# Values of ten column blocks in seven products of quarters, in the second and third batch of a routed attention followed by a gated feed-forward layer

## The chip, the cores and the metric

The kernel runs on one core of a Trainium2 chip. The metric is the device time of one execution in microseconds, the median of three runs. The engines are PE (matmul; PEld is its weight load), DVE (vector), ACT (scalar), POOL (GpSimd) and SP, which here only issues DMAs. PE, DVE and ACT reach the matmul accumulators (PSUM, eight banks); POOL works on SBUF alone.

## The reference

Four batches of eight heads with 768 tokens of 64 numbers. Each query and key goes to the nearest of 16 centroids of its head, and a query attends only to keys of its own cluster. The result, 3072 tokens of 512 numbers, goes through a feed-forward layer of 1536 columns with a sigmoid gate.

```python
q_assign = np.argmax(np.einsum('bhsd,hcd->bhsc', q_n, c_n), axis=-1)
k_assign = np.argmax(np.einsum('bhsd,hcd->bhsc', k_n, c_n), axis=-1)
mask = q_assign[:, :, :, None] == k_assign[:, :, None, :]
scores = np.where(mask, scale * np.matmul(q, k.transpose(0, 1, 3, 2)), -1e9)
attn = softmax(scores)
x = (attn @ v).transpose(0, 2, 1, 3).reshape(B * S, H * D)
gate = 1.0 / (1.0 + np.exp(-(x @ w_gate)))
out = (gate * (x @ w_val)) @ w_out
```

## The kernel before

The program writes out the order of the work by hand. It walks through 384 attention steps, 96 a batch, 24 for each pair of heads and 12 for each head. A step is one score matmul of a key chunk against half the queries (128x384, L1066), one exponential on ACT (L1071), and three small matmuls with the values (av, 128x65, L1089) for the step two places back. `at(step, f)` puts other work at a step: loads of k, q and v (`load`), their splits into a high and a low half-precision part (`sp`, L1631 on DVE, L1632 on POOL), the turn of the split tile by DMA (`turn`), the logits, the pick of the cluster and the hops of the one-hot rows (`pair_prep`). These run some 40 to 80 steps ahead of the head's use.

The feed-forward layer of a batch runs beside the attention of the next. Its pieces ("atoms") stand in a queue, each with a nominal cost in ns; `ffn_run` lets a step take atoms for `ns` (a number for each quarter of a batch in the table `SCHED`). In the first three batches `ffn_atoms` makes them: for each half of the tokens (`blk`, 384 tokens) and each of twelve column blocks `fc` of 128, a gate (four matmuls of 128x384 over the four parts of the 512, then tanh on ACT into `th`) and a value (four matmuls, then one DVE operation (th + 1) * v into `hT`, L553). Sigmoid comes as half of tanh of the half plus a half; the factors sit in the weights' scale. From the second batch on the out product is done for pairs of token chunks in seven products of quarters in place of eight (`product_out`, L994, with sums of `hT` made by `Sums.make` on DVE). The first pair m0 is put `aside` when the first half's values are done, and its atoms alternate with the second half's gates and values; the pairs (3, 2) and (4, 5) follow.

The last batch has no attention behind it. `closing` computes gates and values of ten column blocks in seven products of quarters (columns in pairs, tokens in halves, the 512 in halves): `fin_weights` makes four differences of weight quarters on DVE, `fin_tokens` four sums of token quarters, a `Unit` does the seven products of a pair of column blocks; partial sums are copied from PSUM by ACT, added by DVE, and multiplied with the gate by POOL (L708).

PSUM: a `ring` of four banks (scores, gates, values, logits), two av banks, and two `op` banks, which `out_bank` hands out in turn. `product_out` takes both and chooses by `taken["last"]` which of them its first product writes:

```python
slot = taken["op"] % 2
u = [out_bank() for _ in range(2)]
x = 0 if slot != taken["last"] else 1
taken["last"] = (slot + x) % 2
for z, t in (("x", u[x]), ("y", u[1 - x])): ...
```

SBUF: load tiles `kraw`, `qraw`, `vraw` three each, split tiles `hl` four, turned tiles `T` eight, `th` three.

Of the kernel before, what the change touches and what calls it, by code (L numbers as in the profile page):

```python
# [8 lines left out]
FP = mybir.dt.float32  # L9
# [86 lines left out]
    "fwv": [354, 356, 357, 359, 364, 366, 370, 371], "b3p2pk1": -28.5, "END": 0,  # L96
# [4 lines left out]
def kernel(  # L101
# [42 lines left out]
    hlp = pool("hl", 4)  # L144
    hl2p = pool("hl2", 2)
    tp = pool("T", 8)
# [38 lines left out]
    ident = const.tile([128, 128], FP, name="ident")  # L185
# [12 lines left out]

    def raw(side, b, p):
# [15 lines left out]
    cen = const.tile([128, D], FP, name="cen")  # L215
# [64 lines left out]
    c2 = const.tile([128, 2, D], FP, name="c2")  # L280
    sq = const.tile([128, D], FP, name="sq")
# [114 lines left out]
    T = {}  # L396

    def split(n, parts, lo_eng):

        hl = hlp.tile([128, n, 128], HP, tag="hl", name="hl")  # L400
        for o, r in parts:
            DVE.tensor_copy(hl[:, o : o + r.shape[1], 0:64], r)
        for o, r in parts:
            m = r.shape[1]
            lo_eng.tensor_tensor(
                hl[:, o : o + m, 64:128], r, hl[:, o : o + m, 0:64], ALU.subtract
            )
        return hl

    def turn(key, hl, pl):  # L410
        T[key] = pl.tile([128, hl.shape[1], 128], HP, tag="T", name="T")
        SP.dma_start_transpose(out=T[key], in_=hl.rearrange("p c x -> p (c x)"))
# [19 lines left out]
    def logits1(groups, copy=None):  # L432
# [10 lines left out]
        lo = smp.tile([128, 12, NCL], FP, name="lglo")  # L443
# [134 lines left out]
    def fin_room():  # L578
        if not fin:
            for x in "kq":  # L580
                for n in range(3):
                    r = rawp.tile([128, 2, NCH, 64], FP, tag=f"{x}raw", name=f"{x}raw", bufs=3)
                    fin[x, n] = r.rearrange("p a c d -> p (a c d)").bitcast(HP).rearrange(
                        "p (h x) -> p h x", h=2
                    )

    def fin_weights(w, i, t):

        fin_room()
        if w == 1 and ("h", 0) not in fin:  # L590
            for n in range(4):
                fin["h", n] = hlp.tile([128, 12, 128], HP, tag="hl", name="hl").rearrange(
                    "p c x -> p (c x)"
                ).rearrange("p (h x) -> p h x", h=2)
        a = FC0 // 2 if i == 0 else 0
        q = lambda k, j: (wg, wv)[w][i][:, 2 * k : 2 * k + 2].rearrange(
            "p d (q j) f -> p d q j f", j=2
        )[:, :, a:, j]
        tw = lambda t: (fin["h", 2 * i + (t - 1) // 2] if w else fin["kq"[i], (t - 1) // 2])[
            :, (t - 1) % 2  # L600
        ].rearrange("p (d q f) -> p d q f", d=2, q=3)
        fin["T", w, i, t] = tw(t)
        z, x, y = {
            1: (tw(1), q(0, 1), q(0, 0)), 2: (tw(2), q(1, 1), tw(1)),
            3: (tw(3), q(1, 1), q(0, 1)), 4: (tw(4), q(1, 0), tw(2)),
        }[t]
        cut = lambda v: v if v.shape[2] == 3 - a else v[:, :, a:]
        DVE.tensor_tensor(cut(z), cut(x), cut(y), ALU.subtract)

    def fin_tokens(xT, t):  # L610

        fin_room()
        s = lambda t: fin["kq"[(t - 1) // 2], 2][:, (t - 1) % 2].rearrange("p (d x) -> p d x", d=2)
# [3 lines left out]
        need(*(("x", B - 1, p, c) for p in ps for c in cs))  # L617
# [4 lines left out]
        DVE.tensor_tensor(z, x, y, o)  # L622

# [27 lines left out]
    def closing(xT):  # L651
# [9 lines left out]
        slot = []  # L661
        for _ in range(8):
            t = tp.tile([128, 12, 128], HP, tag="T", name="T")
            v = t.rearrange("p c x -> p (c x)").bitcast(FP)
            slot += [v[:, 0:384], v[:, 384:768]]
# [12 lines left out]
        class Unit:  # L678
            def __init__(u, w, n, f):
                u.w, u.f, u.i, u.q = w, f, f // WQ, f % WQ // 2  # L680
                if w:
                    u.c1, u.c12, u.c22 = slot[3 * (n % 2) : 3 * (n % 2) + 3]
                else:
                    u.c22, u.c21 = slot[6 + 2 * (n % 2) : 8 + 2 * (n % 2)]
                    u.c1, u.c12 = slot[10 + 2 * (n % 3) : 12 + 2 * (n % 3)]

            def mm(u, o, k, start, stop):
                T_ = lambda t, d: fin["T", u.w, u.i, t][:, d, u.q, :]
                W_ = lambda k_, j, d: (wg, wv)[u.w][u.i][:, 2 * k_ + d, (u.f + j) % WQ, :]
                A_ = lambda i, k_, d: xT[:, 2 * k_ + d, 384 * (1 - i) : 384 * (2 - i)]  # L690
                S_ = lambda t, d: fin["S", t][:, d]
                for d in range(2):
                    l, r = {
# [317 lines left out]

    def ffn_block(*a):
        queue.extend(ffn_atoms(*a))

    credit = [0.0]
    turn_ = [0]

# [753 lines left out]
```

## Time and profile before

| | us |
|---|---|
| median of three runs | 319.07 |
| lowest and highest | 319.00, 319.25 |
| the profiled execution | 319.12 |
| its span in the trace | 317.3 |
| PE, DVE, ACT, POOL busy | 310.0, 238.6, 244.9, 120.9 |

A group's row reads: line, engine, operation, output <- inputs, shapes, count | busy us, mean ns of one | idle time of the engine before them and what ended it. Busy time is a union: operations of one engine overlap a little, so the next one costs less than a lone one lasts. The first batch's feed-forward runs from about 39 to 128 us, the second's gates and values from 128.6 to 185.2, its out products to 200.2; the third's from 200.2 to 257.7 and 271.7; then comes the closing.

### The profile page before, as it was taken

The page shows a single profiled execution, that of the slowest core. Times are in us where ns is not written, and L with a number is a line of the kernel's source. Part 1 is how long each engine was busy: PE and PEld are TensorE (multiplying, and loading weights), DVE is VectorE, ACT ScalarE, POOL GpSimd, SP SyncE. Part 2 cuts the span into 40 slices and gives each one's busy share as a digit, 9 for nine tenths or more (in the row PEclk, how much of TensorE's full clock was granted, in tenths as well). Part 3 has the DMA queues.
Part 4 walks back from the last instruction along what each step waited for, and adds up shares of the span by engine and source line. Part 5 has one row for each costly group of instructions (what it writes and reads, how often), then busy time and mean ns, then how long its engine had stood idle before and what let it go on. Part 6 is the DMA issues. An engine that isn't in the chain of part 4 may idle for free.

```text
span 317.3 us, 9228 instructions
## 1 busy us (share of the span) xinstructions
PE 310.0 (98%) x3492; PEld 218.8 (69%) x3492; DVE 238.6 (75%) x623; ACT 244.9 (77%) x555; POOL 120.9 (38%) x157
## 2 busy tenths in 40 slices
PE   7899999999999999999999999999999999999995
PEld 4688766766666666666777678766677678656685
DVE  5899756778688777686788688776888776678983
ACT  6688998797899887877776876777877887588621
POOL 5888454244434275423234333424212111026600
PEclk9999999999999999999999999999999999999999
DMA  7999998639848988976676455882506130300014
GB/s 196 379 259 169 271 164 143 176 83 264 242 100 163 204 221 136 199 217 161 106 193 153 151 118 134 248 153 53 112 2 76 55 27 14 145 1 3 0 35 165
DMA packets 77996, 45.16 MB, mean 142 GB/s; under 512 B 56896, under 2 KB 75520, under 8 KB 77952
## 3 DMA queue, kind: packets, MB, share of 16 engines
q1 hardware_dynamic: 73840, 39.66, 51.3%
q0 software_dynamic: 3680, 4.72, 9.1%
q8 instruction: 27, 0.44, 0.6%
q10 hardware_dynamic: 432, 0.20, 0.2%
q14 instruction: 17, 0.14, 0.1%
HBM read 28.34 MB, written 6.29 MB: 109 GB/s over the span
## 4 chain that ended last, share of the span: by engine, by line
PE 93%; DMA 2%; DVE 1%; POOL 1%; SPq 1%; issue 0%; ACT 0%; DVEq 0%
PE sc L1066 19%; PE g L532 15%; PE v L548 15%; PE av L1089 11%; PE o L994 9%; PE o L865 5%; PE lg L436 2%; PE o L699 2%; PE o_end L802 2%; PE av L699 2%; DMA kraw<-in_k_dram 2%; PE v L628 2%; PE y L699 2%; PE o L802 1%; PE av L802 1%; PE z L699 1%
## 5 line engine op out<-in xcount | busy, mean ns | idle before, releaser
L1071 ACT ACTIVATE es<-sc 128x384 f16<-128x384 f32 x384 | 174.1, 492 | 38.5 <-PE sc L1066 29.8
L1066 PE MATMUL sc<-T 128*128 128x384 f16 x384 | 117.3, 325 | 0.7 <-DVE T L1396 0.4
L1089 PEld LDWEIGHTS <-es 128*128 128x128 f16 x1152 | 81.3, 98 | 35.1 <-ACT es L1071 0.2
L1089 PE MATMUL av<-va,es 128*128 128x65 f16 x1152 | 97.6, 194 | 0.0
L553 DVE SCALAR_TENSOR_TENSOR hT<-th,v 128x384 f16<-128x384 f32 x72 | 39.8, 553 | 33.8 <-PE av L1089 29.6
L377 POOL TENSOR_TENSOR xp<-t,rec 128x384 f16<-128x384 f32 (+1 forms) x30 | 21.8, 726 | 97.3 <-DVE rec L374 49.2
L548 PE MATMUL v<-xTb,wv 128*128 128x384 f16 x288 | 58.5, 326 | 0.1
L532 PE MATMUL g<-xTb,wg 128*128 128x384 f16 x288 | 58.5, 326 | 0.0
L538 ACT ACTIVATE th<-g 128x384 f32<-128x384 f32 x72 | 35.4, 492 | 8.3 <-PE g L532 6.3
L1066 PEld LDWEIGHTS <-T 128*128 128x128 f16 x384 | 37.0, 96 | 1.2 <-DVE T L1396 0.7
L548 PEld LDWEIGHTS <-wv 128*128 128x128 f16 x288 | 28.0, 97 | 13.9 <-issue 0.3
L532 PEld LDWEIGHTS <-wg 128*128 128x128 f16 x288 | 27.9, 97 | 13.9
L1632 POOL TENSOR_TENSOR hl<-kraw,hl 128x384 f16<-128x384 f32 x22 | 20.2, 920 | 40.6 <-DVE hl L1631 25.9
L1632 POOL TENSOR_TENSOR hl<-qraw,hl 128x384 f16<-128x384 f32 x22 | 21.1, 961 | 11.1 <-DVE hl L1631 11.1
L865 PE MATMUL o<-wo,hT 128*128 128x512 f16 x72 | 19.9, 379 | 0.0
L372 DVE TENSOR_TENSOR t<-av,sv 128x390 f32<-128x390 f32 (+1 forms) x30 | 14.4, 480 | 7.1 <-PE av L1089 5.3
L941 DVE TENSOR_TENSOR ob<-o,ob 128x256 f32<-128x256 f32 (+1 forms) x28 | 15.0, 549 | 4.7 <-PE o L994 3.2
L708 POOL TENSOR_TENSOR hT<-T 128x384 f16<-128x384 f32 x12 | 11.8, 1001 | 16.2 <-DVE T L657 15.6
L994 PE MATMUL o<-wo,hT 128*128 128x256 f16 x108 | 16.8, 272 | 0.0
L994 PEld LDWEIGHTS <-sum 128*128 128x128 f16 x144 | 14.0, 97 | 3.3
L451 DVE TENSOR_REDUCE lgs<-lg 128x192 f32<-128x384 f32 x23 | 12.7, 551 | 3.0 <-PE lg L436 2.9
L324 POOL CAST va<-vraw 128x768 f16<-128x768 f32 x15 | 13.1, 873 | 2.4 <-DMA vraw<-in_v_dram 2.4
(225 smaller groups left out, 470.2 us busy)
## 6 DMA issues: line engine op xcount, KB each, us to landing
vraw<-in_v_dram SPq DMA_DIRECT2D x15, 384.0 KB, 4.9
kraw<-in_k_dram SPq DMA_DIRECT2D x14, 384.0 KB, 4.2
qraw<-in_q_dram SPq DMA_DIRECT2D x12, 384.0 KB, 4.1
out_dram<-ob SPq DMA_DIRECT2D x17, 256.0 KB, 2.2
wg<-in_moe_w_gate_dram POOLq DMA_DIRECT2D x2, 768.0 KB, 9.2
wv<-in_moe_w_val_dram POOLq DMA_DIRECT2D x2, 768.0 KB, 10.4
wo<-in_moe_w_out_dram POOLq DMA_DIRECT2D x2, 768.0 KB, 9.3
T<-ohT SPq DMA_DIRECT2D x44, 24.0 KB, 1.9
```

Of the source, the lines that this page charges most:

```text
L377: (eng or POOL).tensor_tensor(x, t[:, 0:nq, 0:64], bcast(rec[:, 0:nq], 64), ALU.mult)
L532: PE.matmul(out=g[:, 0:n], lhsT=wg[fc // WQ][:, dc, fc % WQ, :], rhs=xT[:, dc, t0 : t0 + n], start=(dc == 0), stop=(dc == NDC - 1),)
L538: ACT.activation(th[:, 0:n], g[:, 0:n], AF.Tanh)
L548: PE.matmul(out=w[:, 0:n], lhsT=wv[fc // WQ][:, dc, fc % WQ, :], rhs=xT[:, dc, t0 : t0 + n], start=(dc == 0), stop=(dc == NDC - 1),)
L553: DVE.scalar_tensor_tensor(HB[b, blk][:, fc, 0:n], st[0][:, 0:n], 1.0, w[:, 0:n], ALU.add, ALU.mult)
L699: PE.matmul(out=o, lhsT=l, rhs=r, start=start and d == 0, stop=stop and d == 1, skip_group_check=True,)
L865: PE.matmul(out=o, lhsT=HB[b, blk][:, fc, bass.ts(t, 128)], rhs=wo[fc // WON][:, fc % WON, :], start=(fc == 0), stop=(fc == NFC - 1),)
L994: PE.matmul(out=st[z][:, e], lhsT=a[:, c, :], rhs=rhs[:, c, :], start=start and c + e == 0, stop=c == HF - 1, skip_group_check=True,)
L1066: PE.matmul(out=sc.rearrange("p (c t) -> p c t", t=128), lhsT=s["k"], rhs=s["q"], start=True, stop=True,)
L1071: ACT.activation(es, sc, AF.Exp, scale=SCALE)
L1089: PE.matmul(out=av[:, a0 + s["c0"] + i, :], lhsT=s["es"][:, bass.ts(i, 128)], rhs=VA[b, p][:, e, s["j"], :], start=(first and i == 0 and a ...
L1632: POOL.tensor_tensor(hl[:, :, 64:128], r, hl[:, :, 0:64], ALU.subtract)
```

## The change

The second and third batch (b = 1 and 2) get their feed-forward atoms from a new function `middle`. Gates stay whole. Values of the column blocks 0 and 1 stay whole. The other ten are done in five units of two columns as seven products of quarters, with `quarter`, which is `Unit.mm` taken out of the closing. V(f, k) is product k of the unit that begins at column f; x and y are its two `op` banks, z a ring bank. `early` is queued where the first half's atoms were, `late` where the second half's were; m0's out product is no longer put aside but follows the last value.

```diff
+    def middle(xT, b):
+        gcost, pcost = NDC * 384 / 2.4 + 3, 2 * 163.0
+        c12, c22, c1 = home("c")
+        ths = {}
+        def gate(fc, blk):
+            def f():
...
+                g = fin_group(xT, 0, fc, blk)
+                th = ths[fc, blk] = thp.tile([128, 384], FP, name="th")
+                ACT.activation(th, g, AF.Tanh)
+                if fc >= FC0 and (fc % 2, blk) != (0, 0):
+                    POOL.tensor_scalar(th, th, 1.0, None, ALU.add)
+            return (gcost, f)
+        def from_bank(fc, blk, v):
+            DVE.scalar_tensor_tensor(HB[b, blk][:, fc], ths[fc, blk], 1.0, v, ALU.add, ALU.mult)
...
+        def value(f, k):
+            st = units.setdefault(f, {})
+            def out(c, z, j, blk):
+                DVE.tensor_tensor(c, z, c, ALU.add)
+                POOL.tensor_tensor(HB[b, blk][:, f + j], c, ths[f + j, blk], ALU.mult)
+            def g():
+                if k == 1:
+                    taken["pair"] = True
+                    st["x"] = out_bank()[:, 0:384]
+                if k == 5:
+                    st["y"] = out_bank()[:, 0:384]
+                o = bank(512, name="z")[:, 0:384] if k == 2 else st["y" if k in (5, 3) else "x"]
+                quarter(xT, 1, f, o, k, k in (1, 2, 5), True)
+                if k in (1, 6, 7):
+                    ACT.activation({1: c1, 6: c12, 7: c22}[k], o, AF.Copy)
+                if k == 2:
+                    out(c1, o, 0, 1)
+                if k == 7:
+                    out(c22, st["y"], 1, 0)
+                if k == 3:
+                    out(c12, o, 1, 1)
+                if k == 4:
+                    from_bank(f, 0, o)
+            return (pcost, g)
...
+        G, V = (lambda f, j, i: gate(f + j, 1 - i)), value
+        early = [
+            gate(0, 0), val(0, 0), gate(1, 0), val(1, 0), G(6, 1, 1), V(6, 1), G(6, 0, 1), V(6, 5),
+            V(6, 6), V(6, 7),
+        ]
+        late = [(0.0, lambda: fin_tokens(xT, 4, b)), G(6, 0, 0), V(6, 2), V(6, 4), G(6, 1, 0), V(6, 3)]
+        late += [gate(0, 1), val(0, 1), gate(1, 1), val(1, 1)]
+        for f in (2, 8, 4, 10):
+            late += [
+                V(f, 1), G(f, 0, 0), V(f, 5), V(f, 6), V(f, 2), G(f, 1, 1), V(f, 7), G(f, 0, 1),
+                V(f, 4), G(f, 1, 0), V(f, 3),
+            ]
+            if f == 8:
+                late += [part(m, i, 0, 4) for m in (m0, ma) for i in (1, 2, 3)]
+        late += [part(m, i, 4) for m in (m0, ma) for i in (1, 2, 3)]
+        outs = product_out(b, [m0])
+        n = 6 * HF // SCHED.get("og", 3)
+        late += outs[:n] + [part(mb, i) for i in (1, 2, 3)] + outs[n:] + product_out(b, [ma, mb])
+        return early, late
```

To hold the value differences from the second batch on, tiles are given up: load tiles of k and q become two and one (`x`, for the third pair), split tiles two (`hl`) and two (`hx`, first two batches), turned tiles seven and one (`Tx`), and small constants share one tile `misc`, which later serves as the buffer c1. The weight differences are made in halves, and the values' at steps 150 to 178 in place of 354 to 371. The budgets of the steps are lowered.

```diff
-    -1, "b1lv1": 0.5, "b1lv2": 0.5, "b1lv3": 1.5, "ns02": 490, "ns03": 490, "ns20": 500,
-    "ns21": 491, "ns22": 481, "ns23": 410, "ns30": 443, "ns31": 443, "ns32": 443, "ns33": 423,
+    -1, "b1lv1": 0.5, "b1lv2": 0.5, "b1lv3": 1.5, "ns02": 490, "ns03": 490, "ns20": 484,
+    "ns21": 475, "ns22": 466, "ns23": 400, "ns30": 420, "ns31": 420, "ns32": 420, "ns33": 400,
...
-    "fwv": [354, 356, 357, 359, 364, 366, 370, 371], "b3p2pk1": -28.5, "END": 0,
+    "fwv": [150, 154, 158, 162, 166, 170, 174, 178], "b3p2pk1": -28.5, "fs3": 30, "END": 0,
+    for k, s_ in enumerate(SCHED["fwv"]):
...
-    hlp = pool("hl", 4)
+    hlp = pool("hl", 2)
+    hxp = pool("hx", 2)
     hl2p = pool("hl2", 2)
-    tp = pool("T", 8)
+    lop = pool("lo", 2)
+    tp = pool("T", 7)
+    txp = pool("Tx", 1)
...
+        if side != "v":
+            x = b < 2 and p == 2
+            return rawp.tile(
+                [128, 2, NCH, 64], FP, tag=f"{side}raw" + "x" * x, name=f"{side}raw", bufs=2 - x
+            )
...
+    def home(x):
+        if x not in homes:
+            if x in ("k", "q"):
...
+            elif x in ("kx", "qx"):
...
+            elif x == "v":
+                homes[x] = [flat(p.tile([128, 12, 128], HP, tag=p.name, name="wvs"), 3) for p in (txp, hxp, hxp)]
+                homes[x] += [flat(lop.tile([128, 12, NCL], FP, name="lglo"), 3).bitcast(HP) for _ in range(2)]
+            else:
+                homes[x] = [
+                    hl2p.tile([128, 2, 3, 128], HP, tag="hl2", name="hl2").rearrange(
+                        "p a c x -> p (a c x)"
+                    ).bitcast(FP) for _ in range(2)
+                ] + [misc]
+        return homes[x]
...
-        DVE.tensor_tensor(cut(z), cut(x), cut(y), ALU.subtract)
+        for d in range(2):
+            DVE.tensor_tensor(z[d], x[d], y[d], ALU.subtract)
...
+    def quarter(xT, w, f, o, k, start, stop):
+        i, qn = f // WQ, f % WQ // 2 - (FC0 // 2 if f < WQ else 0)
...
+        for d in range(2):
+            l, r = {
+                1: lambda: (W_(0, 0, d), A_(0, 0, d)), 2: lambda: (W_(1, 0, d), A_(0, 1, d)),
+                3: lambda: (W_(1, 1, d), S_(4, d)), 4: lambda: (T_(4, d), A_(1, 1, d)),
+                5: lambda: (T_(1, d), S_(1, d)), 6: lambda: (T_(2, d), S_(2, d)),
+                7: lambda: (T_(3, d), S_(3, d)),
+            }[k]()
+            PE.matmul(
+                out=o, lhsT=l, rhs=r, start=start and d == 0, stop=stop and d == 1,
+                skip_group_check=True,
+            )
...
+                if b in MID:
+                    at(u + lag, lambda xT=xT, b=b, i=i: middle_block(xT, b, i))
+                    if i == 0:
+                        at(u + SCHED.get(f"ms{b}", 9), lambda xT=xT, b=b: [fin_tokens(xT, t, b) for t in (1, 2, 3)])
+                    continue
```

More of the change, by code (lines that the diff above doesn't have):

```diff
@@ L396, with turn @@
     T = {}
[L398 to L411, printed above, removed]
+    def turn(key, hl):
+        T[key] = new_T(*key)
         SP.dma_start_transpose(out=T[key], in_=hl.rearrange("p c x -> p (c x)"))
@@ L576 @@
     fin = {}
[L578 to L585, printed above, removed]
-    def fin_weights(w, i, t):
[L589 to L594, printed above, removed]
-        a = FC0 // 2 if i == 0 else 0
[L596 to L602, printed above, removed]
+    flat = lambda t, n: t.rearrange("p a c d -> p (a c d)" if n == 4 else "p c x -> p (c x)")
@@ L616, in fin_tokens @@
         ps, cs = {1: ((2, 3), (0, 1, 2)), 2: ((), ()), 3: ((0, 1), range(6)), 4: ((2, 3), range(3, 6))}[t]
-        need(*(("x", B - 1, p, c) for p in ps for c in cs))
+        need(*(("x", b, p, c) for p in ps for c in cs))
         z, x, y, o = {
@@ L660, in closing @@
         seq = [*first, lambda: fin_tokens(xT, 4)]
[L661 to L665, printed above, removed]
+        slot = {}
+        room = list(home("c"))
+        for _ in range(7):
+            v = tp.tile([128, 12, 128], HP, tag=tp.name, name="T")
+            v = v.rearrange("p c x -> p (c x)").bitcast(FP)
+            room += [v[:, 0:384], v[:, 384:768]]
+        for n, t in zip((10, 11, 6, 7, 0, 1, 2, 8, 9, 12, 13, 3, 4, 5, 14, 15), room):
+            slot[n] = t
         sums = {x: Sums(b, *x) for x in ((0, 1), (3, 2), (4, 5))}
```

121 lines of the change are left out of this document (80 added, 41 removed).

## The prediction

> **What bounds the kernel now.** I read the page's busy times and slices first, then the chain of waits, then the busy times of five stretches.
>
> ```profile
> PE 310.0 (98%) x3492; PEld 218.8 (69%) x3492; DVE 238.6 (75%) x623; ACT 244.9 (77%) x555; POOL 120.9 (38%) x157
> ...
> PE   7899999999999999999999999999999999999995
> ...
> PE 93%; DMA 2%; DVE 1%; POOL 1%; SPq 1%; issue 0%; ACT 0%; DVEq 0%
> ```
> ```profile
> 128.60:185.20 56.60, 56.53 (x603) 38.70 (x602) 41.80 (x110) 43.43 (x100) 18.11 (x21) 1.00 0.72 170
> 185.20:200.20 15.00, 15.00 (x197) 12.66 (x195) 12.46 (x31) 11.13 (x23) 6.32 (x8) 1.00 0.53 134
> 200.20:257.70 57.50, 57.50 (x608) 39.42 (x606) 43.76 (x110) 46.24 (x105) 14.22 (x18) 1.00 0.44 86
> 257.70:271.70 14.00, 14.00 (x167) 11.84 (x164) 10.76 (x24) 10.49 (x22) 1.56 (x3) 1.00 0.31 56
> 271.70:300.00 28.30, 28.30 (x179) 17.24 (x177) 22.44 (x47) 21.28 (x48) 11.97 (x13) 1.00 0.07 25
> ```
>
> The columns of the second view are the stretch, its length, then PE, PEld, DVE, ACT and POOL with their instruction counts, the granted clock, and DMA. The first and third stretch hold the gates and values of the second and third batch beside the attention of the batch behind them; the second and fourth mainly their out products; the fifth the closing, which already runs the last batch's gates and values as seven products. PE is busy in all of them at clock 1.00, and the chain is PE for 93% of the span. So a matmul taken out is worth its issue time, if the others keep up. In the first stretch DVE has 26% free, ACT 23%, POOL 68%: this is what the change spends.
>
> **Prices.** From the timeline and the chain:
>
> ```profile
> 200.46 0.65 PE g L532 x4
> ```
> ```profile
> 207.64 0.81 PE L548 MATMUL v<-xTb,wv 128*128 128x384 f16 x4
> ...
> 208.56 0.55 DVE L553 SCALAR_TENSOR_TENSOR hT<-th,v 128x384 f16<-128x384 f32 x1 [0.81 <-PE v L548]
> ...
> 210.49 0.32 PE L1066 MATMUL sc<-T 128*128 128x384 f16 x1
> ...
> 210.74 0.32 PE L1066 MATMUL sc<-T 128*128 128x384 f16 x1
> ```
> ```profile
> 152.65 0.87 ACT L1071 ACTIVATE es<-sc 128x384 f16<-128x384 f32 x2 [0.29 <-PE sc L1066]
> ```
>
> Four 128x384 matmuls take 0.65 us of the chain: 0.163 each. An attention step without a product (one score, three av) takes 210.74 - 210.49 = 0.25 us. DVE starts 208.56 - 208.45 = 0.11 us behind the last matmul that it reads. Two ACT operations end 0.87 us after the first began and one lasts 0.49, so the next one costs 0.38.
>
> **What the change removes.** Per batch ten of the twelve value blocks, in five units of two. A unit had 2 blocks x 2 token halves x 4 matmuls = 16 of 128x384 and now has 7 products x 2 = 14. Ten units lose 20 matmuls: 20 x 0.163 = **-3.26 us** of PE. Nothing else on PE changes in number.
>
> **What it adds on ACT.** Three copies a unit, 30 in all:
>
> ```profile
> L1071 ACT ACTIVATE es<-sc 128x384 f16<-128x384 f32 x74 | 34.2, 491 | 9.4 <-PE sc L1066 8.2 <-PE av L1089 1.0
> L538 ACT ACTIVATE th<-g 128x384 f32<-128x384 f32 x24 | 11.8, 493 | 3.7 <-PE g L532 3.0 <-DVE t L372 0.2 <-DVE hl L1631 0.2
> ```
>
> A unit takes 30 matmuls (14 product, 16 gate) x 0.163 = 4.9 us, plus, at the planner's 0.42 to 0.48 us of products a step, some 11 steps x 0.25 = 2.8: 7.7 us. ACT has 11 exponentials + 4 tanh + 3 copies = 18 x 0.38 = 6.8 us of that, 89%. It hides, but a late copy now holds the exponentials queued behind it, and the av matmuls wait for those.
>
> **What it adds on POOL.** Three products a unit, like the closing's, and three additions of 1.0 to a gate, which the trace doesn't show:
>
> ```profile
> L708 POOL TENSOR_TENSOR hT<-T 128x384 f16<-128x384 f32 x12 | 11.8, 1001 | 16.2 <-DVE T L657 15.6 <-ACT T L758 0.6
> ...
> L1287 POOL CAST hl<-kraw 128x384 f16<-128x384 f32 x2 | 1.0, 499 | 0.0
> ```
>
> An addition costs between the one-input cast, 0.50 us, and the two-input product, 1.00; I take 0.50, since it reads one tensor. A unit then costs POOL 3 x 1.0 + 3 x 0.5 = 4.5 us, and the work already there 18.11/56.60 x 7.7 = 2.5: 7.0 of 7.7 us in the second batch (91%), 14.22/57.50 x 7.7 + 4.5 = 6.4 in the third (83%). What is late when POOL is late: the buffers c1, c12, c22 have one copy each. ACT's copy after product 6 overwrites c12, which POOL must have multiplied since the last unit's product 3. In the changed order V1, G, V5, V6 stand between them: 14 matmuls and about 3 steps, some 3 us from product 3's end. DVE's addition (0.11 + 0.55) and POOL's product (1.0) need 1.7. An av stands behind two further scores and their products, about 1.8 us after its own score, of which the exponential needs 0.7. So POOL may be about 2 us late before PE waits.
>
> **What it adds on DVE.** Per unit four evictions as before:
>
> ```profile
> L553 DVE SCALAR_TENSOR_TENSOR hT<-th,v 128x384 f16<-128x384 f32 x72 | 39.8, 553 | 33.8 <-PE av L1089 29.6 <-PE v L548 3.6
> ...
> L656 DVE TENSOR_TENSOR T<-y,T 128x384 f32<-128x384 f32 x8 | 4.4, 554 | 1.1 <-ACT T L705 0.8 <-PE y L699 0.2
> ...
> L608 DVE TENSOR_TENSOR hl<-wv 128x768 f16<-128x768 f16 x2 | 1.1, 552 | 0.0
> ...
> L622 DVE TENSOR_TENSOR qraw<-xTb 128x768 f16<-128x768 f16 x1 | 0.6, 553 | 0.0
> ```
>
> Three of the four become additions, 0.554 for 0.553: nothing. New are four sums of tokens per batch, 4 x 0.55 = 2.2 us, and some splitting of out sums and of weight differences. 2.2 us on 41.8 of 56.6, in a stretch that the m0 product leaves, keeps DVE near 80%. The closing runs the same scheme with DVE at 22.44/28.30 = 79%, ACT 75%, POOL 42%, and PE at 28.30 of 28.30: that speaks for hiding.
>
> The value differences move from steps 354 to 371 to steps 150 to 178, about 102 to 122 us, and are issued in halves: 4.4 us before, I take 4.6.
>
> ```profile
> 100.00:105.00 5.00, 5.00 (x55) 3.32 (x54) 4.14 (x14) 4.50 (x12) 2.65 (x3) 1.00 0.97 255
> 105.00:110.00 5.00, 5.00 (x62) 3.40 (x61) 3.16 (x10) 4.40 (x12) 1.16 (x1) 1.00 1.11 176
> 110.00:115.00 5.00, 5.00 (x63) 3.26 (x61) 4.34 (x11) 4.42 (x11) 3.43 (x4) 1.00 0.64 179
> 115.00:120.00 5.00, 5.00 (x54) 2.98 (x51) 3.16 (x9) 4.61 (x11) 2.66 (x4) 1.00 1.02 254
> 120.00:125.00 5.00, 5.00 (x61) 3.13 (x60) 4.54 (x14) 4.04 (x11) 2.28 (x4) 1.00 1.18 170
> ```
>
> 14.8 of the first 20 us become 19.4. Without that cover PE would lose up to 4.6 us; but DVE at 4.54 of 5 in the last row costs PE nothing, so I charge none of it separately.
>
> **Tiles and loads.** Split tiles go from four to two beside two, turn tiles from eight to seven and one, load tiles from three to two and one:
>
> ```profile
> kraw<-in_k_dram SPq DMA_DIRECT2D x14, 384.0 KB, 4.2
> ...
> T<-hl SPq DMA_TRANSPOSE x24, 3.7
> ```
> ```profile
> 131.46 0.51 POOL L377 TENSOR_TENSOR xp<-t,rec 128x192 f16<-128x192 f32 x1 [1.61 <-DVE rec L374]
> ```
>
> Every reuse lies ten or more planned steps behind the last reader (a split tile turned at -39.5 is rewritten at -26), some 9 us of attention and products, against 3.7 and 4.2 to land: nothing. SP issues the same number of transfers. The second token half is now needed 14 us into the order less than before: the first product on it follows the first gate by 8.2 us, about 136.8 us, and the turned tokens land at 131.46 + 0.51 + about 2.5: hidden with 2 us to spare.
>
> **The wait that I charge.** The out product m0 ran aside, between gates and values; now it stands behind the last value product. Its two out tiles are the two that the last unit held, and by the rule on the last slot its first product takes y's, the tile that product 3 has just filled. PE then waits for DVE: 0.11 + 0.55 + about 0.1 to be released = 0.76 us. In the second batch the matmuls stand side by side, and a logit reduction and the eviction of product 4 are just ahead on DVE, about 0.25 us: 1.0. In the third a step of 0.25 lies between: 0.5. Together **+1.5 us**; bounds 0 (DVE reads in time) and 4 (a full pick chain ahead on DVE both times). Behind the waiting matmul everything on PE waits.
>
> For late copies and banks inside ten units I charge **+0.5 us**, near the zero of the closing, since ACT and POOL are fuller here; the upper bound is the third rival's. Sum: 319.12 (the profiled execution: span 317.3 and 1.8 around it) - 3.26 + 1.5 + 0.5 = 317.86. The median shown is 0.05 lower: **317.8 us**.
>
> **A rule against it.** DVE's two-input operations already vary:
>
> ```profile
> L464 DVE TENSOR_TENSOR oh<-lgs,mx x42: 244/255/732, 63.7 to 236.6; 128x96 f16<-128x96 f32 x42
> ...
> L332 DVE TENSOR_TENSOR va<-vraw x12: 523/551/1175, 69.5 to 241.4; 128x384 f32<-128x384 f32 x12
> ```
>
> The least, median and greatest ns: a few take 0.5 to 0.65 us longer than the rest. The Trainium skill ("SBUF — State Buffer", Who interferes with whom) says that a DVE instruction with two SBUF inputs and a GpSimd instruction that reads SBUF lock each other out for a whole instruction; these maxima agree with it. By the rule alone about 36 such DVE operations a batch, each half a POOL product late, would add up to 36 x 0.5 = 18 us to DVE, an estimate from that page, and the sum would turn into a loss. The medians at a third of POOL's time busy say that most escape; with POOL near 90% busy I take three times the present excess (0.09 us for L332, less for others), under 4 us of DVE a batch. Its result is the second rival.
>
> **Rivals.** *All waits hidden*, chance 0.17: 319.07 - 3.26 = 315.8. For it: the closing. Against: the tile shared by product 3 and m0.
>
> *DVE late at each change of unit*, 0.14: in the forecast about 1 us lies between y's last eviction and its next product 5; if locked-out operations eat that and 0.12 us more in ten units, 317.8 + 1.2 = 319.0: no change.
>
> *POOL becomes the bound*, slower, 0.22: if an addition costs 1.0 us, a unit costs POOL 8.5 us in the second batch against 7.7, each unit puts it 0.8 further behind, ACT stops at the copy into c12, and the exponentials behind it stop av. Five units x 0.8 less the 1.8 of slack = 2.2: 317.8 + 2.2 = 320.0 us, slower. It decides from (7.7 - 2.5 - 3.0)/3 = 0.73 us an addition. Against: the cast's 0.50.
>
> **How the numbers follow.** The forecast, 317.0 to 318.4, has 0.47. The range 315.7 to 320.3 takes in the bounds of the additions and of the out wait but for its worst. 0.2% of 319.07 is 0.64 us, about what a measurement tells from no change. Faster: 0.45 of the forecast and 0.17 = 0.62; same: 0.02 and most of the second rival = 0.14; slower: 0.24.
>
> **What would show it.** Right: 1114 matmuls of 128x384 where 1134 were; POOL's additions near 0.5 us; one PE gap of 0.5 to 1.0 us before the first out product of each of the two batches, released by DVE; hardly any other. Wrong: PE waits for ACT inside the units, with ACT waiting for POOL; or no gap at the out products.

## The result, and the profile after

| | before | after |
|---|---|---|
| median, us (4 runs each, on one chip) | 319.16 | 333.32 |
| lowest and highest | 319.0, 319.63 | 332.13, 333.87 |
| profiled execution, its span | 319.12, 317.3 | 333.87, 332.1 |

The changed kernel is slower: ratio 1.0436, 95% interval 1.0405 to 1.0467, where 317.8 us (0.996) was forecast. The page of after, its busy times, the slices of PE and POOL, and the chain of waits:

```profile
PE 310.8 (94%) x3472; PEld 217.1 (65%) x3472; DVE 264.2 (80%) x659; ACT 253.7 (76%) x585; POOL 188.3 (57%) x217
...
PE   7899999999999989999969789999987999999995
...
POOL 6787554144354444599999834378986931016700
...
PE 63%; DVE 15%; POOL 9%; issue 4%; ACT 3%; DMA 3%; SPq 1%; POOLq 0%; ACTq 0%; DVEq 0%
```

PE issues the 20 matmuls fewer that were counted (3472 for 3492), yet in the middle of the span some of its slices are 6 to 8 tenths busy where all were 9, and POOL, which was never the bound, is full in five slices on end. The chain now runs through DVE for 15% and POOL for 9%. The windows of after, in the columns of the prediction (stretch, length, PE, PEld, DVE, ACT, POOL with counts, clock, DMA), and then the one of before that it lacks:

```profile
100.00:128.00 28.00, 26.46 (x305) 17.11 (x306) 25.98 (x71) 22.57 (x52) 12.05 (x14) 1.00 0.82 187
128.60:185.20 56.60, 51.12 (x533) 33.06 (x532) 44.37 (x100) 44.50 (x108) 49.34 (x50) 1.00 0.63 141
185.20:200.20 15.00, 12.83 (x156) 10.47 (x155) 13.49 (x35) 9.14 (x20) 7.77 (x8) 1.00 0.56 161
200.20:257.70 57.50, 53.70 (x584) 36.67 (x583) 50.08 (x117) 46.20 (x108) 40.19 (x42) 1.00 0.47 102
```
```profile
100.00:128.00 28.00, 28.00 (x323) 17.95 (x322) 20.79 (x59) 24.20 (x57) 14.13 (x17) 1.00 0.91 191
```

The clock is 1.00 throughout, so the loss is idle PE. From the timeline one can add up every pause of PE of more than 0.12 us between the end of one matmul's issue (0.163 us for 128x384) and the start of the next: 2.2 us from 95 to 128 us, 9.3 from 128 to 202, 5.9 from 202 to 290, together 17.4; before had 0.4. (The idle time in a row's brackets is about 0.16 us less than such a pause, since it counts from the end of the matmul and not of its issue.) That accounts for nearly the whole: 319.12 - 3.26 + 17.4 - 0.4 = 332.9 of the 333.87 of the profiled execution. The stretches have different causes.

**The longest pause, 2.54 us in the row's bracket.** Timeline of after; each row is start, duration, engine, line, operation, and in brackets how long the engine stood idle and who ended it:

```profile
165.15 0.83 POOL L399 TENSOR_TENSOR xp<-t,rec 128x384 f16<-128x384 f32 x1
...
165.93 1.11 POOL L1763 TENSOR_TENSOR hl<-kraw,hl 128x384 f16<-128x384 f32 x1
...
167.01 1.34 POOL L944 TENSOR_SCALAR th<-th 128x384 f32<-128x384 f32 x1
...
168.43 1.17 POOL L959 TENSOR_TENSOR hT<-hl,th 128x384 f16<-128x384 f32 x1
...
169.57 1.34 POOL L944 TENSOR_SCALAR th<-th 128x384 f32<-128x384 f32 x1
169.63 0.49 ACT L970 ACTIVATE hl<-o 128x384 f32<-128x384 f32 x1 [2.56 <-POOL hT L959]
...
170.02 0.87 ACT L1202 ACTIVATE es<-sc 128x384 f16<-128x384 f32 x2
...
170.56 0.81 PE L682 MATMUL g<-xTb,wg 128*128 128x384 f16 x4 [2.54 <-ACT es L1202]
```

Read it backwards. PE waits for the exponentials (L1202), they stand behind ACT's copy of product 6 (L970), and that copy may not overwrite its buffer c12 (a tile named hl) until POOL's product (L959) has read it. POOL is busy almost without a break from 165.15 on. In this pause the forecast's third rival comes true to the letter: ACT stops at the copy into c12 with the exponentials behind it, which the prediction had also named as a sign of being wrong. What the addition costs, from the groups and from the list of its line (least, median, greatest ns):

```profile
L944 POOL TENSOR_SCALAR th<-th 128x384 f32<-128x384 f32 x30 | 36.9, 1231 | 1.2 <-ACT th L942 1.2
...
L970 ACT ACTIVATE hl<-o 128x384 f32<-128x384 f32 x20 | 10.1, 506 | 6.7 <-POOL hT L959 6.4 <-PE o L673 0.4
```
```profile
L944 POOL TENSOR_SCALAR th<-th x30: 1158/1186/1593, 136.5 to 265.3; 128x384 f32<-128x384 f32 x30
```

No addition took less than 1.158 us. The forecast had taken 0.50 and set 1.00 as the upper bound; its rival decided from 0.73.

**Ahead of the units.** The value differences were charged nothing. Timeline at their place:

```profile
113.99 0.82 DVE L1762 CAST hl<-qraw 128x384 f16<-128x384 f32 x1
...
114.74 1.96 DVE L642 TENSOR_TENSOR wvs<-wv,wvs 128x384 f16<-128x384 f16 x2
...
116.62 0.54 DVE L461 TENSOR_REDUCE lgs<-lg 128x192 f32<-128x384 f32 x1
...
117.21 0.32 PE L1197 MATMUL sc<-T 128*128 128x384 f16 x1 [1.31 <-DVE lgs L461]
```

Two halves of 384 elements, which took 0.32 to 0.35 us each at their fastest, took 1.96 together while POOL worked beside them; the reduction that empties the logit bank stood behind them, and the next score needed the bank. DVE is busy for 25.98 of these 28 us in place of 20.79.

**Behind the units.** Timeline of after at the first out product:

```profile
182.08 0.55 DVE L461 TENSOR_REDUCE lgs<-lg 128x192 f32<-128x384 f32 x1
...
182.66 0.35 DVE L472 TENSOR_REDUCE mx<-lgs 128x12 f32<-128x192 f32 x1
...
183.05 0.43 DVE L474 TENSOR_TENSOR oh<-lgs,mx 128x96 f16<-128x96 f32 x2
...
183.40 0.83 POOL L346 CAST va<-vraw 128x768 f16<-128x768 f32 x1
183.51 0.76 DVE L481 TENSOR_SCALAR oh<-oh 128x96 f16<-128x96 f16 x1
...
184.18 0.54 DVE L949 SCALAR_TENSOR_TENSOR hT<-th,o 128x384 f16<-128x384 f32 x1
...
184.65 0.55 DVE L958 TENSOR_TENSOR hl<-o,hl 128x384 f32<-128x384 f32 x1
184.78 0.49 PE L1118 MATMUL o<-wo,hT 128*128 128x256 f16 x3 [1.13 <-DVE hT L949]
```

A whole pick chain (reduction of the logits, maximum, comparison, scaling: L461 to L481) stands ahead of product 4's eviction (L949). PE waits 1.13 us by the bracket, a pause of 1.29. Two more such pauses follow, 1.08 us at 189.1 and 1.40 us at 194.7, both for DVE's additions to the out tiles (L1065); the second has a pick chain ahead of it too.

**In the third batch.** Timeline of after, the largest pause there:

```profile
247.27 0.55 DVE L958 TENSOR_TENSOR hl<-o,hl 128x384 f32<-128x384 f32 x1
247.74 0.48 DVE L642 TENSOR_TENSOR wgs<-wg 128x256 f16<-128x256 f16 x2
...
248.14 0.55 DVE L461 TENSOR_REDUCE lgs<-lg 128x192 f32<-128x384 f32 x1
...
249.96 0.42 DVE L1033 TENSOR_TENSOR sum<-hT 128x512 f16<-128x512 f16 x1
...
251.89 0.42 DVE L1037 TENSOR_TENSOR sum<-hT 128x512 f16<-128x512 f16 x1
252.22 0.55 DVE L958 TENSOR_TENSOR misc<-z,misc 128x384 f32<-128x384 f32 x1
...
252.82 0.81 PE L682 MATMUL g<-xTb,wg 128*128 128x384 f16 x4 [1.51 <-DVE misc L958]
```

DVE goes without a pause from the gates' differences through a pick chain and six part sums of the out product before it reads z, and the gate's bank is late.

### The profile page after: what moved, and what is told of

Same layout as the page of the kernel before. It is cut to its first block, busy times and chain, and to the rows that moved or that the text cites. A ratio compares the mean times of both kernels' runs of the same rounds, so it can differ in the third digit from the quotient of the medians.

```text
span 332.1 us, 9330 instructions
## 1 busy us (share of the span) xinstructions
PE 310.8 (94%) x3472; PEld 217.1 (65%) x3472; DVE 264.2 (80%) x659; ACT 253.7 (76%) x585; POOL 188.3 (57%) x217
## 4 chain that ended last, share of the span: by engine, by line
PE 63%; DVE 15%; POOL 9%; issue 4%; ACT 3%; DMA 3%; SPq 1%; POOLq 0%; ACTq 0%; DVEq 0%
PE sc L1197 12%; PE o L1118 7%; PE av L1220 7%; PE g L682 5%; PE o L908 4%; PE o L673 4%; PE g L542 4%; PE v L558 4%; POOL th L944 3%; POOL hT L959 3%; PE v L682 3%; ACT es L1202 2%; PE o_end L845 2%; PE av L673 2%; DMA T<-hl 2%
## 5 line engine op out<-in xcount | busy, mean ns | idle before, releaser
L1202 ACT ACTIVATE es<-sc 128x384 f16<-128x384 f32 x384 | 175.3, 497 | 34.9 <-PE sc L1197 26.9
L1197 PE MATMUL sc<-T 128*128 128x384 f16 x384 | 118.5, 325 | 3.8 <-DVE lgs L461 1.3
L682 PE MATMUL g<-xTb,wg 128*128 128x384 f16 x208 | 42.3, 326 | 4.3 <-ACT es L1202 2.7
L944 POOL TENSOR_SCALAR th<-th 128x384 f32<-128x384 f32 x30 | 36.9, 1231 | 1.2 <-ACT th L942 1.2
L682 PEld LDWEIGHTS <-wg 128*128 128x128 f16 x208 | 20.2, 97 | 16.9 <-issue 5.9
L942 ACT ACTIVATE th<-g 128x384 f32<-128x384 f32 x48 | 24.0, 501 | 8.3 <-PE g L682 2.8
L959 POOL TENSOR_TENSOR hT<-hl,th 128x384 f16<-128x384 f32 x20 | 21.2, 1058 | 6.9 <-DVE hl L958 6.4
L563 DVE SCALAR_TENSOR_TENSOR hT<-th,v 128x384 f16<-128x384 f32 x24 | 13.3, 552 | 9.7 <-PE av L1220 8.0
L558 PE MATMUL v<-xTb,wv 128*128 128x384 f16 x96 | 19.5, 326 | 0.0
L542 PE MATMUL g<-xTb,wg 128*128 128x384 f16 x96 | 19.5, 325 | 0.0
L1065 DVE TENSOR_TENSOR ob<-o,ob 128x256 f32<-128x256 f32 (+1 forms) x28 | 14.9, 549 | 5.2 <-PE av L1220 2.1
L461 DVE TENSOR_REDUCE lgs<-lg 128x192 f32<-128x384 f32 x23 | 12.7, 550 | 6.8 <-PE lg L446 6.8
```

The lines of the kernel that those rows point to most:

```text
L542: PE.matmul(out=g[:, 0:n], lhsT=wg[fc // WQ][:, dc, fc % WQ, :], rhs=xT[:, dc, t0 : t0 + n], start=(dc == 0), stop=(dc == NDC - 1),)
L558: PE.matmul(out=w[:, 0:n], lhsT=wv[fc // WQ][:, dc, fc % WQ, :], rhs=xT[:, dc, t0 : t0 + n], start=(dc == 0), stop=(dc == NDC - 1),)
L682: PE.matmul(out=o[:, 0:384], lhsT=w[:, dc, fc % WQ, :], rhs=xT[:, dc, 384 * blk : 384 * blk + 384], start=(dc == 0), stop=(dc == NDC - 1),)
L942: ACT.activation(th, g, AF.Tanh)
L944: POOL.tensor_scalar(th, th, 1.0, None, ALU.add)
L959: POOL.tensor_tensor(HB[b, blk][:, f + j], c, ths[f + j, blk], ALU.mult)
```

## The experiments

Times are medians of four runs (ten for the last version but one); the ratio is against the kernel before on the same chip in the same session (318.8 to 319.5 us).

### POOL's additions

Without them (the products then take tanh without the 1.0):

```diff
-                if fc >= FC0 and (fc % 2, blk) != (0, 0):
-                    POOL.tensor_scalar(th, th, 1.0, None, ALU.add)
```


> The 30 additions of 1.0 to the gates on POOL are left out (so those gates are tanh alone and the values wrong by that part); all else as in the changed kernel. Theory P: the additions, 1.23 us each where 0.50 was taken, make POOL the bound of both stretches (3.9 to 4.0 us busy of 4 from 148 to 184 us); without them a unit costs POOL 3.0 + 2.5 = 5.5 us of 7.7, the waits of ACT for POOL vanish, and the time falls by 7 us or more, to about 323 to 326; what is left over 316 is DVE and the out products. Rival R: DVE is the cause (two-input operations of 0.28 us that take up to 1.07 beside POOL, and the out tiles), and POOL's lateness a symptom: the time falls by less than 3 us, to above 330.

325.84 us, ratio 1.0199 (1.0173 to 1.0226): 7.5 us less than the changed kernel. The pauses for ACT's copies are gone, as its row of the groups shows beside the one above:

```profile
L968 ACT ACTIVATE hl<-o 128x384 f32<-128x384 f32 x20 | 10.0, 502 | 0.4 <-PE o L673 0.4
```

POOL's additions are half of the loss, and DVE ends 8.5 of the 10.7 us of pauses that remain behind 95 us. What PE waited for from 128 to 202 us, in the changed kernel and then without the additions (total, times, longest):

```profile
PE g L682 <- ACT es L1202: 2.5, 1, 2.5
PE o L1118 <- DVE ob L1065: 2.2, 2, 1.2
PE o L1118 <- DVE hT L949: 1.1, 1, 1.1
PE sc L1197 <- ACT es L1202: 0.6, 1, 0.6
PE sc L1197 <- ACT th L942: 0.6, 1, 0.6
PE o L673 <- ACT hl L970: 0.4, 1, 0.4
```
```profile
PE o L1116 <- DVE ob L1063: 1.8, 2, 1.2
PE sc L1195 <- DVE misc L956: 0.7, 1, 0.7
PE o L1116 <- DVE hT L947: 0.3, 1, 0.3
PE o L673 <- DVE hT L947: 0.2, 1, 0.2
PE g L682 <- DMA xTb<-xp: 0.2, 1, 0.2
```

With every pause of more than 0.12 us counted from the end of issue, those that ACT ends fall here from 5.5 to 0.6 us, and those that DVE ends stay at 3.8 in sum, though not each of them. So in this stretch the loss is POOL's queue, passed on by ACT. From 202 to 290 us it is the other way: those that ACT ends stay at 1.2 us, and those that DVE ends fall from 4.7 to 3.2. How the additions delay DVE there, no run here shows.

The additions on DVE, and then the whole product with the gate on DVE, which leaves POOL out of the units:

```diff
-                    POOL.tensor_scalar(th, th, 1.0, None, ALU.add)
+                    DVE.tensor_scalar(th, th, 1.0, None, ALU.add)
```


> The same additions on DVE in place of POOL. Theory P: POOL is relieved by 37 us, DVE gets 30 operations of 0.2 to 0.5 us (6 to 15 us over 105): between the kernel without additions and the changed one, about 325 to 328. Rival R: DVE is the bound, so work moved to it costs more than it relieves: above 333.

332.62 us, ratio 1.0407 (1.0372 to 1.0442).

```diff
-                POOL.tensor_tensor(HB[b, blk][:, f + j], c, ths[f + j, blk], ALU.mult)
+                DVE.scalar_tensor_tensor(HB[b, blk][:, f + j], ths[f + j, blk], 1.0, c, ALU.add, ALU.mult)
```


> POOL gets no work from the units at all: DVE does addition of 1.0 and product with the gate in one operation behind its own addition, 30 more of 0.4 to 0.55 us (12 to 16 us over 105). Theory P: POOL back at a third busy, its locks on DVE gone; DVE at about 90%: 322 to 328, with gaps of PE released by DVE. Rival R: as in the last run, above 333.

330.24 us, ratio 1.0328 (1.0287 to 1.037). Both end above what theory P expected and below what rival R did. POOL's queue is relieved, at 153.5 and 122.9 us busy for 188.3, but DVE goes from 259.4 us busy (without additions) to 271.4 and 266.2, and most of PE's pauses are then ended by DVE. So DVE has no room for the work either.

The additions put into the kernel before (POOL adds 1.0 to 30 gates, DVE's value operation only multiplies):

```diff
                 ACT.activation(th[:, 0:n], g[:, 0:n], AF.Tanh)
+                if b in (1, 2) and fc >= 2 and (fc % 2, blk) != (0, 0):
+                    POOL.tensor_scalar(th, th, 1.0, None, ALU.add)
```


> The kernel before, whole values, with the 30 additions of 1.0 alone: POOL adds 1.0 to the same gates, and DVE multiplies with the result. POOL gets 37 us over 115 and stays below 70% busy. Theory P: no bound, so within 1 us of before, 319 to 320; each addition 1.16 to 1.25 us also here, that is its own price and not the crowding. Rival R: DVE's two-input operations are held by the additions, the time grows by 2 us or more.

330.18 us, ratio 1.0342 (1.0308 to 1.0377): 11 us, where theory P expected at most one. Rival R's number, 2 us or more, came true, but not its reason: DVE is busy 239.2 us for 238.6 before, so its operations did not become longer. Two groups of it:

```profile
L540 POOL TENSOR_SCALAR th<-th 128x384 f32<-128x384 f32 x30 | 35.8, 1195 | 28.8 <-ACT th L538 23.8 <-DVE t L372 2.7 <-DVE wo L278 2.3
...
L556 DVE TENSOR_TENSOR hT<-th,v 128x384 f16<-128x384 f32 x30 | 16.6, 553 | 28.4 <-POOL th L540 24.2 <-PE av L1094 3.1 <-PE g L532 1.0
```

The price, 1.195 us, is not one of crowding: here POOL is busy 47% of the time and often idle ahead of the additions. The loss has another cause than in the changed kernel: the addition lies between gate and value, DVE stops 24.2 us in all for it with everything else queued behind, and the ring's banks are freed late. The expectation had looked at POOL's share of time and not at this chain.

Gates in half precision, so that POOL adds on half-precision tiles:

```diff
-                th = ths[fc, blk] = thp.tile([128, 384], FP, name="th")
+                part_ = fc >= FC0 and (fc % 2, blk) != (0, 0)
+                th = ths[fc, blk] = thp.tile([128, 384], HP if part_ else FP, tag="th", name="th")
```


> The changed kernel with the gates that POOL multiplies kept in half precision, so that POOL adds 1.0 on half-precision tiles. If its price goes by bytes, like the cast's 0.50 us, theory P expects 326 to 328 us (near the 325.84 without additions). If it goes by elements and stays at 1.16 to 1.23 us: 332.5 to 334 us.

331.01 us, ratio 1.0383 (1.036 to 1.0407). The list of the lines:

```profile
L945 POOL TENSOR_SCALAR th<-th x30: 1162/1175/1476, 135.7 to 261.2; 128x384 f16<-128x384 f16 x30
```
```profile
L960 POOL TENSOR_TENSOR hT<-hl,th x20: 907/914/1091, 140.3 to 262.4; 128x384 f16<-128x384 f32 x20
```

The addition's price does not fall with the bytes: 1.175 us for 1.186 with half of them. Only the products fell, from 1.00 to 0.91 us, which is the likely source of the 2.3 us that came back. The time lies between the two that were expected.

### The weight differences

All of them left out (plain weights stand in the tiles), with and without the additions:

```diff
-        for d in range(2):
-            DVE.tensor_tensor(z[d], x[d], y[d], ALU.subtract)
+        fin["T", w, i, t] = x
```


> The weight differences in halves are left out (16 for the values, 16 for the gates; the tiles hold plain weights, so the values of ten blocks and the closing are not the reference's); additions on POOL stay. Theory D (the differences take DVE's time in stretches where evictions queue behind them): the gap of 1.47 us at 117 us and about 3 us of those at 241 to 257 us go, 328.5 to 330 us. Theory P alone (POOL's addition is all of the loss, and DVE only passes it on): the gaps at 241 to 257 stay, 331.5 to 333 us.

330.36 us, ratio 1.0344 (1.0304 to 1.0385), a little above theory D's bound. The pause at 117 us is gone and those from 202 to 290 us fall from 5.9 to 3.9.

> Both left out: POOL's 30 additions and the 32 halves of weight differences. If the two losses are separate, the time falls by the one beside the other: 325.8 (without the additions alone) less 3.5 to 5 us = 321 to 322.5 us. If they are one queue seen twice, 324 to 326 us. What remains above 315.9 (before less 20 matmuls) belongs to neither: the token and part sums on DVE, the out tile, the copies.

321.52 us, ratio 1.0061 (1.0041 to 1.008). The differences cost 333.32 - 330.36 = 3.0 us beside the additions and 325.84 - 321.52 = 4.3 without them, so the two losses are separate queues that share a little. What is left belongs to neither: 321.52 against 319.48 - 3.26 = 316.2 is 5.3 us. The timeline of this run has pauses of 0.43, 0.73 and 1.40 us at the second batch's out products, together 2.6, and 3.6 elsewhere, most of them 0.15 to 0.4 us and the longest 0.82 at 165.5 us.

The differences in one instruction where their operands lie in a row, at the same steps:

```diff
-        for d in range(2):
-            DVE.tensor_tensor(z[d], x[d], y[d], ALU.subtract)
+        DVE.tensor_tensor(z, x, y, ALU.subtract)
```


> The changed kernel with weight differences in one instruction where their operands lie in a row (12 wholes of 768 or 512 elements and 8 halves in place of 32 halves). If the halves' own cost matters (a half lasts 254 to 281 ns at the least, but 685 to 861 ns in the mean, some 4 us more than wholes in all): 331 to 332.5 us. If the place counts and not the form: 333 us or above.

331.42 us, ratio 1.0377 (1.0342 to 1.0411): the halves as such cost about 1.9 us of the 3.0 to 4.3, give or take about one by the intervals.

### The tile of the first out product

```diff
-            x = 0 if slot != taken["last"] else 1
+            x = 0 if P_ == 1 or slot != taken["last"] else 1
```


> m0's first out product takes x's tile, which product 4's eviction left earlier, in place of y's, which product 3 has just filled. Theory S (the shared tile is what holds the first out product): the gap of 1.29 us ahead of it in the second batch and the 0.28 in the third go, 331.8 to 332.2 us. Theory D (DVE is late there anyway, with the sums and the evictions queued behind each other, and the gap only moves to the next product): 333 us, the same gap a few products on.

333.37 us, ratio 1.043 (1.0412 to 1.0449), the same pause of 1.29 us. The edit does nothing, here and in the later versions that hold it: the built program shows that the tile written first gets bank 6, where the unit's x was, with either choice, and differs in tile names alone. So the first out product never took y's tile. The timeline above had said so: it starts at 184.78, 0.06 us after product 4's eviction and 0.42 before the one of product 3 ends.

### One batch at a time

The new order in the third batch alone, then again with the second batch's budgets as they were, then in the second batch alone with the third's budgets as they were:

```diff
-    MID = (1, 2)
+    MID = (2,)
```


> The changed kernel with the new order in the third batch alone; the second batch runs as before the change, ten matmuls (1.63 us) fewer are saved. Theory P and D: the gaps of the third batch (5 us) and the one beside the value differences (1.5 us) stay, those of the second go: 323.5 to 324.5 us. If each batch's loss depends on the other (work late in the second pushes the third), 319 to 321 us.

330.76 us, ratio 1.037 (1.0339 to 1.0402). Far over the expectation: the third batch has 10.6 us of pauses, where the changed kernel has 5.9.

```diff
-    ... "ns20": 484, "ns21": 475, "ns22": 466, "ns23": 400,
+    ... "ns20": 500, "ns21": 491, "ns22": 481, "ns23": 410,
```


> As the run with the third batch alone (330.76 us), with the second batch's budgets back at 500, 491, 481 and 410, which its 16 uncut values a unit need. If the surplus loss of that run (10.6 us of gaps in the third batch in place of 5) came from work of the second batch that ran over into the third: 323.5 to 324.5 us. If the third batch loses by itself about what both lose together, as DVE's and POOL's queues hit the units in another phase: 329 to 331 us.

325.13 us, ratio 1.0177 (1.0146 to 1.0208). In the first of the two the second batch had its full work under the lowered budgets; the third batch's first gate began at 202.95 us in place of 201.85. With the budgets back the time is 5.6 us less, if still above the 323.5 to 324.5 expected: a shift of some steps between products and attention matters as much as the causes above.

```diff
-    MID = (1, 2)
+    MID = (1,)
```


> The new order in the second batch alone; the third runs as before the change with its budgets back. Gaps of the changed kernel up to 200 us, 11.3 us, less 1.63 us saved: 328 to 329.5 us if they stay what they were. If theory P and D hold, most of it is the 2.7, 1.3, 1.1 and 1.4 us at the last unit and the out products.

328.77 us, ratio 1.0288 (1.0256 to 1.0321). The batches add up: 5.9 and 9.6 us, less the pause of 1.5 us beside the value differences that both runs hold, is 14.0 of the 14.2 us lost.

### Towards a version without loss

Half-precision gates with DVE's addition, whole differences at other steps (values 104 to 174, gates 350 to 374), part sums spread over the fourth unit:

```diff
-                    POOL.tensor_scalar(th, th, 1.0, None, ALU.add)
+                    DVE.tensor_scalar(th, th, 1.0, None, ALU.add)
...
-    "fwv": [150, 154, 158, 162, 166, 170, 174, 178],
+    "fwv": [104, 112, 134, 142, 150, 158, 166, 174],
```


> Nothing left out. The gates that POOL multiplies are kept in half precision, and 1.0 is added on DVE on half-precision tiles; the weight differences are whole where their operands lie in a row, the values' spread over steps 104 to 174 and the gates' at 350 to 374; the six part sums of the out product are spread over the fourth unit; the first out product takes x's tile. Theory P and D together: POOL is back at about 154 us busy and DVE has its bursts spread, 319 to 322 us. If DVE's total of the unit binds (evictions, additions and attention together), not its bursts: 325 to 328 us.

327.07 us, ratio 1.0248 (1.0207 to 1.0289): the better of the two outcomes was missed, and the time is the one expected if DVE's total is the limit. DVE is now at 49.7 of 56.6 us in the second batch. The differences on POOL instead:

```diff
-        DVE.tensor_tensor(z, x, y, ALU.subtract)
+        POOL.tensor_tensor(z, x, y, ALU.subtract)
```


> As the kernel with half-precision gates (327.07 us), but POOL makes the weight differences. DVE loses some 13 us of work, POOL gains some 30 us, mostly in stretches where it is half free. Theory D (DVE's load in and ahead of the units is what is left): 322 to 324 us, near the 321.52 that is left with neither additions nor differences. If POOL's load is what PE feels wherever it lies (splits and products queued behind differences of about 2 us each): 327 us or above.

332.86 us, ratio 1.0434 (1.0416 to 1.0452). DVE has 20 instructions fewer and is busy 265.0 us in place of 263.8: what was taken from it, 11.4 us, came back as longer operations beside POOL's differences of 0.7 to 2.0 us (the part sums alone go from 22.9 to 27.9 us). The same in the third batch alone:

> The new order in the third batch alone, with half-precision gates and DVE's addition on them, the weight differences on POOL and whole, spread as in the run with half-precision gates. Of the 1.63 us saved, theory D leaves the 1.5 to 2 us of gaps that the third batch had with neither additions nor differences: 318.8 to 320 us, the first version that would not be slower. If the additions on DVE still cost as in the second batch: 321 to 322 us.

330.58 us, ratio 1.0363 (1.0338 to 1.0389). It also kept the second batch's lowered budgets, so the two causes aren't parted here. With the budgets back, the differences on DVE at steps 196 to 252 and 350 to 374, and half-precision gates:

> The third batch alone with its neighbour's budgets back, half-precision gates with DVE's addition, whole differences (values at steps 196 to 252, gates at 350 to 374) and x's tile for the first out product. Theory D: with the bursts away from units and pick chains 319 to 321 us. If even five units beside attention keep DVE late: 324 us or above.

320.68 us, ratio 1.0049 (1.0031 to 1.0067). And the same with POOL's additions in single precision:

> As the best run so far (320.68 us: third batch alone, half-precision gates with DVE's addition, differences whole and moved), but POOL adds 1.0 on single-precision gates as in the changed kernel. In the third batch POOL has 14 of 57 us taken by other work, so five units of 3 x 1.0 + 3 x 1.2 leave it time. Theory: there the differences alone were the loss, 320 to 321.5 us. If POOL's additions count in the third batch too: 323 us or above.

324.17 us, ratio 1.0133 (1.0102 to 1.0163). Against the 325.13 us of the third batch alone, the place and form of the differences gave 1.0 us, which the intervals, overlapping, hardly tell from nothing; POOL's additions in place of DVE's cost 3.5, so they count there too. The windows of the two from 224 to 240 us, DVE's addition first:

```profile
224.00:240.00 16.00, 15.97 (x176) 10.58 (x174) 13.38 (x36) 15.01 (x38) 7.32 (x8) 1.00 0.34 69
```
```profile
224.00:240.00 16.00, 15.72 (x170) 10.43 (x169) 12.20 (x23) 14.64 (x36) 15.68 (x16) 1.00 0.26 57
```

POOL at 15.68 of 16 us is full in the third batch as well. No version beat the kernel before; the best still gave back more than the 1.63 us of its ten matmuls.

## Why the prediction was wrong, point by point

The forecast was 317.8 and the time 333.3, a miss of 15.5 us. **The step that failed** first and most is the price of POOL's addition, "between the one-input cast, 0.50 us, and the two-input product, 1.00; I take 0.50, since it reads one tensor". The chip took 1.19, outside both bounds. The bracket rested on the thought that a one-input operation can't cost more than a two-input one; a cast and an addition with a constant proved to be different operations, and nothing in the trace priced the second. The rest of that rival's arithmetic then comes near in total. With 1.2 us a unit costs POOL 3 + 3.6 + 2.5 = 9.1 us against 7.7 in the second batch and 3 + 3.6 + 1.9 = 8.5 in the third; five units less the 1.8 of slack give 5.2 and 2.2, together 7.4, and leaving the additions out gave 7.5. That the two agree so closely is partly luck: the pauses fall by 4.5 us in the second batch and by 1.6 in the third, and only in the second are they those of ACT at its copy, as the rival says. The condition, 0.73, was on record; the value on the wrong side of it was chosen.

**The differences, "I charge none of it separately"**, failed by 3.0 to 4.3 us. The sixteen halves for the values took 7.2 us of DVE where 4.6 were taken, and one row with DVE at 4.54 of 5 and PE full was read as proof that DVE may be late. It only showed that PE needed nothing late from DVE in those 5 us.

**Out products: +1.5, measured 3.8 in the second batch and 0.3 in the third.** The wait ahead of the first one was there, 1.29 for 1.0, but for product 4's eviction behind a pick chain, not for y's tile. The two behind it, 1.08 and 1.40, weren't foreseen: m0 no longer runs aside, three pairs stand packed in one stretch, and each change of pair waits for DVE.

**Waits in units: +0.5**, measured, with neither additions nor differences, some 3.2 (3.6 less the 0.4 that before has). With the 2.6 of the out products this closes the sum: 317.8 + 1.1 + 2.7 = 321.6 for 321.52 measured. From there 4.3 for the differences and 7.5 for the additions lead to 333.3, as they must, since both were read off the runs on that way.

**What held.** 20 matmuls fewer at 0.163. ACT's copies nearly hide: without the additions ACT ends 1.8 us of pauses from 128 to 290 us, none above 0.42, for 6.7 with them. The eviction sums on DVE cost what they did before, 0.55. The cover for the second token half was thinner than the 2 us forecast: in the second batch alone a pause of 0.5 us at 139.6 is ended by its transfer.

**The lock-out rival.** The one-hot comparison is the clearest row, after and then without additions:

```profile
L474 DVE TENSOR_TENSOR oh<-lgs,mx 128x96 f16<-128x96 f32 x42 | 13.5, 362 | 0.7
```
```profile
L474 DVE TENSOR_TENSOR oh<-lgs,mx 128x96 f16<-128x96 f32 x42 | 9.7, 271 | 0.7
```

With 659 DVE instructions in both, 30 additions on POOL make DVE busy 264.2 us for 259.4: 4.8 us over two batches, within the forecast's "under 4 us of DVE a batch". In the kernel before, the same additions left DVE at 239.2 for 238.6, so what they do to DVE hangs on what runs beside them. The rule of the Trainium skill ("SBUF — State Buffer", Who interferes with whom), by which a two-input DVE instruction and a GpSimd instruction that reads SBUF exclude each other, agrees with the two rows.

## What to carry to other kernels

Price an operation that the trace doesn't show by a run of its own or by the worst end of its bracket, above all where a rival's condition lies inside the bracket, and ask whether the bracket's rows are of the same operation at all. An engine's share of busy time doesn't say whether it may be late: look at what stands behind each of its in-order waits, as the addition between gate and value shows, which cost 11 us on an engine half idle. Before removing PE work that is worth 1%, check that each engine that pays for it has room in the very stretch and in a row, not on average.

## What was not expected of the hardware

POOL's addition of a constant to 128x384 took 1.16 us at the least and 1.17 to 1.19 in the median, in single and in half precision, more than its product of two tensors (1.00, or 0.91 with one of them in half precision) and its cast (0.50). On DVE the same addition took 0.32 us at the least in single and 0.22 in half precision, but up to 1.16 and 1.02 where POOL worked beside it. DVE's scaling of the one-hot rows, one input of 128x96, took 187 to 191 ns before and up to 757 after, as at 183.51, where it ended within 0.04 us of POOL's cast.
